# Backward pass of a recurrent memory attention: dV's and dK's sum folded into dQ's bank, and a shorter set-up of the backward loop

## The chip, the cores and the metric

The kernel runs on one core of a Trainium2 chip. The metric is the device time of one execution in microseconds (us). TensorE (PE in the profile) multiplies matrices, with weight loads listed apart as PEld; VectorE (DVE), ScalarE (ACT) and GpSimd (POOL) do elementwise work; SyncE (SP) and GpSimd issue most of the DMAs. SBUF is the on-chip memory, and PSUM holds the results of TensorE.

## The reference

A layer with adaptive layer norms, an attention over segments with a carried memory, and a gated feed-forward network; the kernel returns its output and eleven gradients. What matters here is the attention. 2048 rows of 512 are cut into 64 segments of 32 rows. Each segment sees 8 memory rows and its own 32, and its first 8 output rows are the next segment's memory:

```python
for s in range(n_seg):
    h = concatenate([mem, xs], axis=1)                  # 40 rows of 512
    q, k, v = (einsum('btd,dhe->bhte', h, W) for W in (Wq, Wk, Wv))   # 32 heads of 128
    p = softmax(where(mask, einsum('bhqe,bhke->bhqk', q, k) * scale, -1e9))
    o = einsum('bhte,hed->btd', einsum('bhqk,bhke->bhqe', p, v), Wo)
    mem = o[:, :M, :]
    outs.append(o[:, M:, :])
```

The backward pass walks the segments from 63 down to 0. For each it needs dO from dy and Wo, then dV, dP, dS, dK and dQ, and from these the gradient of the 40 input rows, dh = dV Wv^T + dK Wk^T + dQ Wq^T. The first 8 rows of dh are the gradient of the memory, and so a part of dy of the segment that is handled next. That makes the loop a chain.

## The kernel before

`phase4` is the backward loop over the 64 segments, the stretch from about 1513 to 2500 us of the profile. The order of all engines' instructions in the loop is the order of the program text (`pin`). The heads lie three to a group of 128 columns, in 11 groups, of which 120 columns are used: three times 32 rows, then three times the last 8 rows of the 40. Columns 120 to 127 of each group are padding.

One segment goes like this. `col_pass` multiplies dy (`dyT`) with `WoT` into `pass_ps`, which is copied to `RAd`; eight transposes (`turn_ps`) bring it to `dOT`. GpSimd also copies `RAd` to rows 0 to 95 of `dOst` (L1693). Rows 96 to 119 of `dOst` are dO of the last 8 rows of each head. These come from `RBd`, which holds dO of the last 8 rows of four segments, by three small DMAs on GpSimd's queue (`dO_tails`, L1579). Then come the products for dV, dP, dS, dK and dQ (`g_ps`, `dp_ps`, `tps`).

The sum dh is made in two banks of PSUM. `dht` puts the products of dV with `WvT` and of dK with `WkT` into `dh_ps`, 128 x 512. Each head's product fills a strip of 32 partitions (the first 32 rows of the 40), four heads side by side, so that the four strips have still to be added. `dht_pairs` puts those of dQ with `WqT` into `dhq_ps`, 128 x 256: here two strips hold the left half of the 512 columns and two the right half. `pair_mm` issues four such matmuls at a time, one for each strip. Both banks are split into two bf16 tiles, a high part on ScalarE and the remainder on VectorE, so that TensorE can add the strips without loss: `fold_split` puts the parts of `dh_ps` into the tile `dST` (L312, L313), and `split_pair` makes `dh_hi` (L230) and `dh_lo` (L232) from `dhq_ps`. `fold_sum` (L323) then adds everything into `dh_ft`, 128 x 4 x 32, which is dh transposed: eight matmuls for the parts of `dh_ps` with the selector `foldsel` (it adds four strips), eight for those of `dhq_ps` with `foldhalf` (it adds two). ScalarE copies the memory rows of `dh_ft` to the next `dyT` (L1767), and the next segment's `col_pass` can begin.

Between the split and the fold stands other work of TensorE where there is some: a piece of the product of the last 8 rows of four segments (`TailRows`, `dh_tps`), of 16 or 24 matmuls, from the fifth segment of the loop on. In one segment of four, eight matmuls of that product's own fold (`dh_b_ft`) follow it, also at L323.

Before the loop, tiles are cleared. `ptiles` clears whole tiles with GpSimd memsets (L1463): `dS`, `dOst`, `dKT`, `dQT`, `Qst` and `Kst`, 128 x 1408 each. VectorE clears `dOT` (L1468). SP loads `OT`, `Pst` and `VT` of segments 63 and 62 (L1547, L1550), and `Qst` and `Kst` of segment 63 once these are cleared (L1564). GpSimd goes on with `to_heads` (L65), which writes the last rows into `dOT`; then the three DMAs of `dO_tails`, a DMA of eight zero rows to `DHA` (L1582), and the first copies to `dOst`. The scheduler chooses the place of what stands outside the pinned loop.

Of the kernel before, what the change touches and what calls it, by code (L numbers as in the profile page):

```python
# [40 lines left out]
class K:  # L41
# [1389 lines left out]
    def phase4(self):  # L1431
        nc, tc, cfg, io = self.nc, self.tc, self.cfg, self.io
        D, DC, H, E, L, M, T, G, NS = cfg.D, cfg.DC, cfg.H, cfg.E, cfg.L, cfg.M, cfg.T, cfg.G, cfg.NS
        GW = 128
# [4 lines left out]
        with self.p4_ctx as ctx:  # L1439
# [6 lines left out]
            psp = ctx.enter_context(tc.tile_pool(name="p4ps", bufs=6, space=PSUM, reuse_waits="tile"))  # L1446
# [11 lines left out]
            def ptiles(name, n, zero=True):  # L1458
                ts = []
                for i in range(n):  # L1460
                    t = pt.tile([128, G * GW], BF16, name=f"{name}{i}")
                    if zero:
                        nc.gpsimd.memset(t[:], 0.0)  # L1463
                    ts.append(t)
                return ts
# [3 lines left out]
            RAd = pt.tile([128, 8 * 128], BF16, name="RAd")  # L1469
            RBds = [pt.tile([128, 8 * 128], BF16, name=f"RBd{i}") for i in range(2)]  # L1470
            btd = pt.tile([128, 8, 128], BF16, name="btd")
            dSs = ptiles("dS", 1)
            dSTs = ptiles("dST", 1, zero=False)
            dOst_t = ptiles("dOst", 1)[0]
            dXTs = {nm: ptiles(nm, n, zero=nm != "dVT") for nm, n in (("dVT", 1), ("dKT", 1), ("dQT", 1))}

            def part3(t, pi):
                return t[:, pi * PW:min((pi + 1) * PW, G * GW)].rearrange("p (g x) -> p g x", x=GW)
# [17 lines left out]
            def to_heads(eng, src, i0, n, r0, w, o):  # L1496

                b = 0 if w == 32 else 96
                s4 = src.rearrange("p i (j r) -> p i j r", r=32)
                d = dOT[:, 120 * i0:120 * (i0 + n)].rearrange("p (i x) -> p i x", x=120)[:, :, b:b + 3 * w]  # L1500
                self.evac(eng, d.rearrange("p i (j r) -> p i j r", r=w), s4[:, :, 0:3, o:o + w])
                for g in range(3):
                    lo, hi = max(3 * g, i0), min(3 * g + 3, i0 + n, 8)
                    if lo < hi:
                        d = dOT[:, 960 + 120 * g + b + w * (lo - 3 * g):960 + 120 * g + b + w * (hi - 3 * g)]
                        self.evac(eng, d.rearrange("p (i r) -> p i r", r=w), s4[:, lo - i0:hi - i0, 3, o:o + w])
# [9 lines left out]
            def proj_b(t, hf, parts=1):  # L1516
                ps = psb.tile([128, 512], F32, name="pass_ps", tag="dh")

                def part(k):
                    self.col_pass(psp, WoT, hf, lambda c: dbs[t][:, c, :, :].rearrange("p s q -> p (s q)"), None, None, ps,  # L1520
                                  range(k * DC // parts, (k + 1) * DC // parts))

                part(0)

                def rest():
                    for k in range(1, parts):
                        part(k)
                    return lambda: self.evac(("act", "dve")[hf], RBds[t % 2][:, 512 * hf:512 * hf + 512], ps[:])

                return rest  # L1530

            def turn_b(t):
                tps = [self.turn_half(psp, RBds[t % 2], hf) for hf in range(2)]

                def f():
                    for hf in range(2):
                        self.evac(("act", "dve")[hf], btd[:, 4 * hf:4 * hf + 4, :], tps[hf][:])
                return f
# [31 lines left out]
            get_loads(NS - 1)  # L1570
            for hf in range(2):
                proj_b(NS // 4 - 1, hf)()()
            turn_b(NS // 4 - 1)()
            to_heads("pool", btd[:], 0, 8, 32, 8, 24)

            def dO_tails(s):
                for j in range(3):
                    o = 32 * j + 8 * (s % 4)
                    nc.gpsimd.dma_start(dOst_t[96 + 8 * j:104 + 8 * j, 0:1024], RBds[(s // 4) % 2][o:o + 8, :])  # L1579

            dO_tails(NS - 1)
            nc.gpsimd.dma_start(self.DHA[NS, 0:M, :], dSs[0][0:M, 0:D])  # L1582
            nseg_t = 128 // T
            row_stores = []

            def store_rows_x(left):
                while len(row_stores) > left:
                    row_stores.pop(0)()
# [3 lines left out]
            i0 = len(self.traced())  # L1592
            for s in reversed(range(NS)):
# [12 lines left out]
                dS, dST, dOst = dSs[0], dSTs[0], dOst_t  # L1606
                dVT, dKT, dQT = dXTs["dVT"][0], dXTs["dKT"][0], dXTs["dQT"][0]
# [74 lines left out]
                def dht_pairs(X, WT):  # L1682
                    ps = psp.tile([128, 256], F32, name="dhq_ps", tag="p")
                    off = lambda h: (h // 3) * GW + (h % 3) * 32
                    for n in range(H // 2):
                        hs = (2 * n, 2 * n + 1)
                        self.pair_mm(ps, [X[:, off(h):off(h) + 32] for h in hs], [WT[:, h, :] for h in hs], n, H // 2)
                    return ps

                for a, n, eng in ((0, 4, "dve"), (4, 2, "act"), (6, 2, "act")):  # L1690
# [66 lines left out]
                dht(dVT, WvT, 2)  # L1757
                parts = self.fold_split(sb2, dh_ps[0], "dh", dST)
                pair = self.split_pair(sb2, dht_pairs(dQT, WqT), "dh")
                tail.collect(s % nseg_t, [dVT, dKT, dQT])  # L1760
                tail.chunk()
                if split:
                    self.pop_later()
                store_rows_x(2)
                ft = self.fold_sum(psp, parts, "dh", "p", pair)
                if dyT_next is not None:
                    nc.scalar.activation(dyT_next[:, :, 0:M], ft[:, :, 0:M], AF.Copy)  # L1767
                g = s // 4
# [428 lines left out]
```

## Time and profile before

| | us |
|---|---|
| median of three runs | 3073.68 (3072.13 to 3074.03) |
| the profiled execution, its own time | 3071.52 |
| its span, first to last instruction | 3069.7 |
| TensorE busy in the span | 2972.8 |
| VectorE, ScalarE, GpSimd busy | 1604.4, 1285.6, 1212.6 |
| mean granted clock of TensorE | 0.991 |

The span and what lies around it (1.8 us) make the profiled execution's time, which is 2.16 us below the median of the runs. In the lists of the trace, a line gives the start in us, the duration, the engine and the line of the kernel, the operation with out<-in, the shape, the count, and in brackets the idle time of the engine before it with what ended that time. Neighbours of one kind are merged into one line (x16 is 16 instructions), whose duration runs from the first start to the last end. The chain lists only what set the end: each step follows from what released it.

### The profile page before, as it was taken

The page shows a single profiled execution, that of the slowest core. Times are in us where ns is not written, and L with a number is a line of the kernel's source. Part 1 is how long each engine was busy: PE and PEld are TensorE (multiplying, and loading weights), DVE is VectorE, ACT ScalarE, POOL GpSimd, SP SyncE. Part 2 cuts the span into 40 slices and gives each one's busy share as a digit, 9 for nine tenths or more (in the row PEclk, how much of TensorE's full clock was granted, in tenths as well). Part 3 has the DMA queues.
Part 4 walks back from the last instruction along what each step waited for, and adds up shares of the span by engine and source line. Part 5 has one row for each costly group of instructions (what it writes and reads, how often), then busy time and mean ns, then how long its engine had stood idle before and what let it go on. Part 6 is the DMA issues. An engine that isn't in the chain of part 4 may idle for free. (4 is left out here: it accounts for less than half of the span.)

```text
span 3069.7 us, 106628 instructions
## 1 busy us (share of the span) xinstructions
PE 2972.8 (97%) x44289; PEld 1859.2 (61%) x44289; DVE 1604.4 (52%) x3746; ACT 1285.6 (42%) x3179; POOL 1212.6 (40%) x2640
## 2 busy tenths in 40 slices
PE   6999999999998899989899999999999999999999
PEld 3666666666665444445567777777777754445454
DVE  5556656656655788732255555555555532322221
ACT  2555555555555433322255555555555520111011
POOL 2554555555544222211244444444444422333321
PEclk8999999999999999999999999999999999999999
DMA  9887887887887899997599999999999998666574
GB/s 303 216 220 203 219 212 208 210 217 208 213 207 253 197 229 231 226 285 242 169 246 245 245 244 247 246 248 246 244 246 252 247 280 270 205 197 220 184 243 143
DMA packets 839319, 703.53 MB, mean 229 GB/s; under 512 B 539730, under 2 KB 711794, under 8 KB 837940
## 3 DMA queue, kind: packets, MB, share of 16 engines
q1 hardware_dynamic: 713668, 486.69, 62.9%
q0 software_dynamic: 54512, 148.63, 15.5%
q10 hardware_dynamic: 70656, 61.41, 6.4%
q8 instruction: 348, 5.70, 0.8%
q14 instruction: 135, 1.11, 0.1%
HBM read 294.93 MB, written 276.35 MB: 186 GB/s over the span
## 5 line engine op out<-in xcount | busy, mean ns | idle before, releaser
L1987 PE MATMUL gps<-rows,hrows 128*128 128x512 bf16 (+2 forms) x2160 | 417.5, 355 | 0.0
L1987 PEld LDWEIGHTS <-hrows 128*128 128x128 bf16 x2160 | 211.2, 98 | 204.6
L1693 POOL COPY dOst<-RAd 96x512 bf16<-96x512 bf16 x128 | 75.1, 611 | 309.3 <-DVE RAd L63 309.3
L63 DVE CAST ot<-gps 128x512 bf16<-128x512 f32 (+3 forms) x76 | 48.1, 633 | 284.2 <-PE gps L1987 192.5
L656 PE MATMUL pass_ps<-Wv,hT 128*32 128x512 bf16 (+2 forms) x2304 | 188.2, 357 | 0.0
L61 ACT ACTIVATE ot<-gps 128x512 bf16<-128x512 f32 (+3 forms) x75 | 41.3, 551 | 350.6 <-PE gps L1987 228.0
L255 PEld LDWEIGHTS <-hT 128*32 128x32 bf16 x4096 | 125.1, 97 | 95.8 <-DMA Wq<-in_A_Wq_dram 6.2
L1991 POOL DMA_DIRECT2D out_dram<-ot x108 | 81.3, 753 | 251.0 <-DVE ot L63 134.0
L942 POOL TENSOR_TENSOR Pst<-Pst,rden 120x1408 bf16<-120x1408 bf16 x63 | 159.8, 2537 | 39.1 <-issue 23.3
L61 ACT ACTIVATE dVT<-g_ps 128x480 bf16<-128x480 f32 (+1 forms) x192 | 104.7, 545 | 97.1 <-PE g_ps L1649 96.6
L63 DVE CAST Vst<-pass_ps 96x512 bf16<-96x512 f32 x128 | 87.3, 682 | 107.4 <-ACT RBv L61 97.7
L215 PE MATMUL dh_ps<-WvT,dVT 128*32 128x512 bf16 x2048 | 133.6, 381 | 0.1
L255 PE MATMUL pass_ps<-Wq,hT 128*32 128x512 bf16 x2048 | 125.6, 383 | 6.0 <-DMA Wq<-in_A_Wq_dram 6.0
L2001 PE MATMUL gps5o<-WoT,rows 128*128 128x512 bf16 x592 | 128.3, 379 | 1.6 <-DMA rows<-OSR 1.6
L223 PE MATMUL at_ps<-Wo,OT 128*32 128x256 bf16 x4096 | 124.8, 275 | 2.6 <-DMA Wo<-in_A_Wo_dram 2.6
L656 PE MATMUL pass_ps<-Wv,hb 128*32 128x512 bf16 (+2 forms) x636 | 127.2, 345 | 0.0
L255 PE MATMUL pass_ps<-Wk,hT 128*32 128x512 bf16 x2048 | 124.3, 380 | 1.7 <-POOL hT L545 1.1
L731 POOL DMA_DIRECT2D Vst<-RBv x192 | 99.4, 523 | 64.6 <-ACT ET L778 39.9
L255 PE MATMUL pass_ps<-WoT,dyT 128*32 128x256 bf16 (+1 forms) x3072 | 122.4, 308 | 0.9 <-ACT dyT L1767 0.9
L223 PE MATMUL dhq_ps<-WqT,dQT 128*32 128x256 bf16 x4096 | 122.9, 273 | 0.0
L215 PE MATMUL dh_ps<-WkT,dKT 128*32 128x512 bf16 x2048 | 122.3, 380 | 0.0
L223 PEld LDWEIGHTS <-dQT 128*32 128x32 bf16 x4096 | 109.7, 97 | 15.7
(413 smaller groups left out, 7004.2 us busy)
## 6 DMA issues: line engine op xcount, KB each, us to landing
OSR<-Ost SPq DMA_DIRECT2D x64, 352.0 KB
OT<-OT SPq DMA_DIRECT2D x64, 352.0 KB
VT<-VTr SPq DMA_DIRECT2D x64, 352.0 KB
PS<-Pst SPq DMA_DIRECT2D x64, 352.0 KB
OT_l<-OT SPq DMA_DIRECT2D x64, 352.0 KB
Pst_l<-PS SPq DMA_DIRECT2D x64, 352.0 KB
VT_l<-VT SPq DMA_DIRECT2D x64, 352.0 KB
DVR<-rows_x POOLq DMA_DIRECT2D x64, 352.0 KB, 6.0
```

The lines of the kernel that those rows point to most:

```text
L61: return nc.scalar.activation(out, in_, AF.Copy)
L63: return nc.vector.tensor_copy(out, in_)
L215: self.nc.tensor.matmul(ps[32 * j:32 * j + 32, :], lhsT=lhsT, rhs=w, start=(n < 4), stop=(n >= total - 4), tile_position=(0, 32 * j))
L223: nc.tensor.matmul(ps[32 * j:32 * j + 32, :], lhsT=x[k], rhs=w[k][:, 256 * d:256 * d + 256], start=(n == 0), stop=(n == total - 1), tile_p ...
L255: self.nc.tensor.matmul(ps[32 * j:32 * j + 32, :], lhsT=lhs(c), rhs=rhs, start=(c == 0), stop=(c == DC - 1), tile_position=(0, 32 * j))
L656: nc.tensor.matmul(ps[32 * j:32 * j + 32, o * E:(o + n) * E], lhsT=lhsT, rhs=wc[:, 3 * a + hl:3 * (a + n - 1) + hl + 1:3, :], start=(c == ...
L731: nc.gpsimd.dma_start(Vst[96 + 8 * j:104 + 8 * j, :], rb[32 * j + o:32 * j + o + 8, :])
L942: nc.gpsimd.tensor_tensor(Pst[0:120, :, :], Pst[0:120, :, :], rden[:, :].unsqueeze(2).to_broadcast([120, G, 128]), op=ALU.mult)
L1693: nc.gpsimd.tensor_copy(dOst[0:96, 512 * hf:512 * hf + 512], RAd[0:96, 512 * hf:512 * hf + 512])
L1987: nc.tensor.matmul(ps[:, 0:ng * E], lhsT=hrows[:, tp_, c * 128:(c + 1) * 128], rhs=rows[:, tp_, 0:ng * E], start=(tp_ == 0), stop=(tp_ == ...
L1991: nc.gpsimd.dma_start(outw[c * 128:(c + 1) * 128, h0:h0 + 3 * (ng - 1) + 1:3, :], ot[:, 0:ng * E].rearrange("p (h e) -> p h e", e=E))
L2001: nc.tensor.matmul(pss[gg][:], lhsT=src[0][:, src[1], gg * E:(gg + 1) * E], rhs=dyrows[:, tp_, :], start=(tp_ == order[0]), stop=(tp_ == o ...
```

## The change

The four products of `foldsel` with the two parts of `dh_ps` now go into `dhq_ps`, as a seventeenth round of `pair_mm` behind the sixteen of dQ. The split of `dhq_ps` thus holds the whole sum, and `sum_pair` folds it with eight matmuls in place of sixteen. Before the loop, `dS`, `dKT` and `dQT` are no longer cleared as a whole, only at their padding columns (and `dS` at the rows that the zero rows of `DHA` are read from); `dOst` is cleared by VectorE; and `dO_tails` is moved ahead of `turn_b` and `to_heads`, with GpSimd's order pinned there. In the built program, SP's loads of `Qst` and `Kst` then stand third and fourth, ahead of the first load of `VT`.

```diff
-            dSs = ptiles("dS", 1)
+            dSs = ptiles("dS", 1, zero=False)
             dSTs = ptiles("dST", 1, zero=False)
-            dOst_t = ptiles("dOst", 1)[0]
-            dXTs = {nm: ptiles(nm, n, zero=nm != "dVT") for nm, n in (("dVT", 1), ("dKT", 1), ("dQT", 1))}
+            dOst_t = ptiles("dOst", 1, zero=False)[0]
+            nc.vector.memset(dOst_t[:], 0.0)
+            dXTs = {nm: ptiles(nm, n, zero=False) for nm, n in (("dVT", 1), ("dKT", 1), ("dQT", 1))}
+            nc.vector.memset(dSs[0][0:32, 0:D], 0.0)
+            for t in (dSs[0], dXTs["dKT"][0], dXTs["dQT"][0]):
+                nc.vector.memset(t[:].rearrange("p (g x) -> p g x", x=GW)[:, :, 120:GW], 0.0)
...
-            turn_b(NS // 4 - 1)()
-            to_heads("pool", btd[:], 0, 8, 32, 8, 24)
...
+            i0 = len(self.traced())
             dO_tails(NS - 1)
+            turn_b(NS // 4 - 1)()
+            to_heads("pool", btd[:], 0, 8, 32, 8, 24)
             nc.gpsimd.dma_start(self.DHA[NS, 0:M, :], dSs[0][0:M, 0:D])
+            self.pin(i0, [mybir.EngineType.Pool])
...
                     for n in range(H // 2):
                         hs = (2 * n, 2 * n + 1)
-                        self.pair_mm(ps, [X[:, off(h):off(h) + 32] for h in hs], [WT[:, h, :] for h in hs], n, H // 2)
+                        self.pair_mm(ps, [X[:, off(h):off(h) + 32] for h in hs], [WT[:, h, :] for h in hs], n, H // 2 + 1)
+                    self.pair_mm(ps, [self.foldsel[:, :]] * 2, parts, H // 2, H // 2 + 1)
                     return ps
...
-                ft = self.fold_sum(psp, parts, "dh", "p", pair)
+                ft = self.sum_pair(psp, pair, "dh", "p")
```

`sum_pair` exists already:

```python
ft = psp.tile([128, self.cfg.DC, 32], F32, name=name + "_ft", tag=tag)
for i in range(2):
    for c in range(self.cfg.DC):
        self.nc.tensor.matmul(ft[:, c, :], lhsT=parts[i][:, (c % 2) * 128:(c % 2) * 128 + 128],
                              rhs=self.foldhalf[:, c // 2, :], start=(i == 0 and c == 0), stop=(i == 1),
                              skip_group_check=True)
```

## The prediction

> **What bounds the kernel now.** I read the page first, then the chain of the backward loop, then the list of instructions at the end of one segment, and last the list and the DMA view of the loop's start.
>
> ```profile
> PE 2972.8 (97%) x44289; PEld 1859.2 (61%) x44289; DVE 1604.4 (52%) x3746; ACT 1285.6 (42%) x3179; POOL 1212.6 (40%) x2640
> ```
>
> TensorE is busy for 97% of the span, twice any other engine. In the loop it hardly ever waits; the chain of a segment's end is TensorE alone:
>
> ```profile
> 1702.60 1.75 PE dhq_ps L223 x64
> 1704.34 0.86 PE dh_tps L215 x16
> 1705.21 0.50 PE dh_ft L323 x16
> 1705.70 2.71 PE pass_ps L255 x64
> ```
>
> So what changes TensorE's own work here is paid or saved in full, unless the split of `dhq_ps` (ScalarE, then VectorE) becomes later than TensorE's other work. Both are in the list of the same segment:
>
> ```profile
> 1703.34 0.69 DVE L313 TENSOR_TENSOR dST<-dh_ps,dST 128x512 bf16<-128x512 f32 x1 [2.42 <-ACT dST L312]
> ...
> 1704.17 1.04 PE L215 MATMUL dh_tps<-WqT,dh_tail 128*32 128x512 bf16 x16
> 1704.40 0.38 ACT L230 ACTIVATE dh_hi<-dhq_ps 128x256 bf16<-128x256 f32 x1 [1.09 <-PE dhq_ps L223]
> ...
> 1705.45 0.25 PE L323 MATMUL dh_ft<-foldsel,dh_lo 128*128 128x32 bf16 x4
> ...
> 1705.63 0.62 PE L255 MATMUL pass_ps<-WoT,dyb 128*32 128x512 bf16 x8
> ```
>
> From the start of `dh_hi` to the next pass it takes 1.23 us. The loop's first segment, which has no `dh_tps` in between, shows how short that can get when the split alone decides: 1.09 us.
>
> ```profile
> 1539.51 0.38 ACT L230 ACTIVATE dh_hi<-dhq_ps 128x256 bf16<-128x256 f32 x1 [1.09 <-PE dhq_ps L223]
> 1539.93 0.42 DVE L232 TENSOR_TENSOR dh_lo<-dhq_ps,dh_hi 128x256 bf16<-128x256 f32 x1 [0.78 <-ACT dh_hi L230]
> ...
> 1540.41 0.27 PE L323 MATMUL dh_ft<-foldsel,dh_lo 128*128 128x32 bf16 x4 [0.19 <-DVE dh_lo L232]
> ...
> 1540.60 0.61 PE L255 MATMUL pass_ps<-WoT,dyb 128*32 128x512 bf16 x8
> ```
>
> At the loop's start TensorE stands still for 8 us, and the three DMAs of `dO_tails` end it:
>
> ```profile
> 1513.45 1.27 POOL L1463 MEMSET dS<- 128x1408 bf16 x1 [0.32 <-PE wtp L1400]
> ...
> 1514.04 0.61 DVE L1468 MEMSET dOT<- 128x664 uint32 x1
> ...
> 1519.51 1.27 POOL L1463 MEMSET Kst<- 128x1408 bf16 x1
> ...
> 1520.81 0.33 SPq L1564 DMA_DIRECT2D Kst<-KST  x1
> ...
> 1521.84 1.53 POOL L1579 DMA_DIRECT2D dOst<-RBd  x3
> ...
> 1527.48 0.56 PE L1649 MATMUL g_ps<-Pst_l,dOst 128*128 128x120 bf16 x4 [7.99 <-DMA dOst<-RBd]
> ```
>
> **The fold, segment by segment.** Removed are 8 of 16 fold matmuls. In the list they start 0.025 us apart (four `dh_hi` and four `dh_lo` starts lie 0.10 apart), so TensorE saves 8 x 0.025 = 0.20 us. Added are four products of 32 x 256, in the form of the 64 before them; 64 take 1.75 us, so one round of four takes 1.75 / 16 = 0.11 us. No product of `foldsel` with 256 columns is in the trace; its bounds are 0.11 us if the four strips work abreast like dQ's, and 4 x 0.11 = 0.44 us if they go one after another. I take 0.11, the row of the same shape and strips. TensorE's own work falls by 0.09 us.
>
> The split starts later by the same 0.11 us, as it now waits for the extra round. That has to fit in the room between TensorE's path and the split's. With a `dh_tps` of 16 and nothing more, the room is 1.23 - 1.09 = 0.14 us, of which 0.11 are used: the segment gains 0.04 (0.146 - 0.110 with the starts to the ns), not 0.09. Where eight matmuls of `dh_b_ft` or eight more of `dh_tps` stand between, there are over 0.2 us more room and the segment gains 0.09. Of four segments two are of each sort: 2 x 0.036 + 2 x 0.09 = 0.25 us. 60 segments have such work: 15 x 0.25 = 3.8 us less. The first four have none, and there the later split costs its 0.11 in full: 0.4 us more. **The loop gains 3.3 us.**
>
> The new wait is that the second product needs VectorE's part in `dST` (L313). It ends at 1704.03 in the list. The round before the products begins at 1704.06 and they follow 0.11 later, at 1704.17, which leaves 0.14; with 0.06 from an end on VectorE to the matmul that waits for it (1540.35 to 1540.41), 0.08 to 0.09 us are left. The figure is the same to 0.01 in all 64 segments. Behind it would queue everything of TensorE; a delay beyond 0.09 us costs its length in each segment.
>
> The other engines do the same as before. SP's and GpSimd's queues in the loop are unchanged, and q1, the hardware queue of SP's loads, is empty for some 3 us of each segment (1713.0 to 1716.0 for instance, by the packets), so a segment shorter by 0.06 us finds its loads in time. If that cover were gone, at most the 3.3 us would be lost.
>
> **The start.** Removed from GpSimd are four memsets of 1.27 us at 1.21 distance, 4.9 us. VectorE takes on the clearing of `dOst` (128 x 704 against `dOT`'s 128 x 664 in 0.61: 0.65 us), of 32 x 256 in `dS` (0.24 by the same rate), and three padding strips of 44 elements (0.04 by that rate, at most the 0.21 of a 128 x 128 copy of that engine): 1.0 to 1.5 us. VectorE has 1.07 us free between the memset of `dOT` and the copy to `RBd` at 1515.72, so `RBd` is later by 0 to 0.4 us; behind it queue `turn_ps`, `btd` and the first pass, all of them ahead of the 8 us of idle time that covers this. GpSimd would clear `Qst` and `Kst` by 1515.9, start `dO_tails` when `RBd` is whole, at about 1516.7, issue the last of the three at 1517.7, and have `to_heads` (1.2 us), the zero rows (0.5) and the copies to `dOst` (1.2) done by 1521.1. By issue times alone the tails are 5.1 us sooner.
>
> What they gain depends on how the DMA engines order them. SP's loads of `Qst` and `Kst` wait for the memsets and are now issued about 4.8 us earlier, so that all eight loads of 330 to 352 KB are in the queue before the last tail is. The rows that bear on it are the stores of `DKR` and `DQR`, of one size and from the same queue as the tails:
>
> ```profile
> DKR<-rows_x POOLq DMA_DIRECT2D x58, 352.0 KB, 5.2
> DQR<-rows_x POOLq DMA_DIRECT2D x58, 352.0 KB, 3.6
> ...
> dOst<-RBd POOLq DMA_DIRECT2D x174, 16.0 KB, 5.0
> ```
>
> The `DKR` issued at 1709.11 is behind three loads of SP (1706.2 to 1709.0), and its first packet starts at 1712.9, 3.8 us later, just as the last packet of those loads is served; the `DQR` issued at 1713.94 finds q1 empty, and its first packet starts 1.1 us later. At the loop's start it is the same: one DMA engine of the sixteen works off loads without a break, 0.112 us a packet, until 1526.37, and serves the tails' semaphores from 1526.38 on, though the other engines had them from 1523.1. So DMAs are served here nearly in the order of arrival, and the tails stay last. The bytes ahead of them are the same as before; only the pauses before `Qst` and `Kst` (under 1 us for a usual engine, none for the slowest) fall away. By this the gain lies between -0.5 (another engine is slow) and 1.5 us; I take 0.8.
>
> The Trainium skill says otherwise ("DMA: Bandwidth & Descriptors", "Queues, rings and completion order"): each DMA engine takes turns between the queues that have work, packet by packet. By this rule the tails would pass the loads, and the sum would be 7.6 us less in place of the 4.1 of the rows; the `DKR` row speaks against it, and the rows decide here.
>
> TensorE's granted clock adds scatter to the start: it is 0.50 from 1521.17 to 1531.41, so 3.9 us of work after the wait run at half speed, and 2 us are lost. The clock's changes lie on a grid of 3.41 us (10.24 is three steps), and where the wait ends on that grid is chance. I leave this loss as it is, and give the range 1 us for it.
>
> **Sum.** 3.3 + 0.8 = 4.1 us less. The profiled execution would go from 3071.52 to 3067.4; against the median of 3073.68 it is 3069.6 us. What a measurement of this kernel can tell from no change is about 0.2%, 6.1 us, so the forecast is a gain below that bound.
>
> **Rivals.** First, the tails pass the loads. Then they land some 2 us after their issue (a store issued at 1512.59 into an empty queue landed at 1514.55), by about 1520.7; the copies to `dOst` end at 1521.1, and next late is `VT`, now the fifth load, whose last share would come when the fifth load's came before, at 1523.4. The start gains 4.3 us in place of 0.8: 3073.68 - 3.3 - 4.3 = 3066.1 us. The 5.0 us of the tails' usual landing speak against it. Chance 0.24.
>
> Second, the later split eats the gain in more segments than I count, by a fold that restarts more slowly after a wait, or by 0.05 us more at the first product. Then the loop gains nothing: 3072.9 us. The room of 0.036 us in half the segments speaks for it. Chance 0.11.
>
> Third, slower: the four products do not run abreast, as all four carry one stationary matrix. They then take 0.44 us: TensorE's path grows by 0.24 us in 30 segments, the split's by 0.29 in 30 and 0.44 in four: 7.2 + 8.7 + 1.8 = 17.7 us more, 3090.6 with the start's gain. It decides from 0.05 us a segment on, where the 3.3 us are used up. Against it: dQ's own rounds use one matrix for two strips and show 0.11. Chance 0.10, with any other loss.
>
> **How the numbers follow.** The forecast keeps 0.55. The range goes from the first rival with the clock's scatter, 3065.3, to the second, 3073.6; it leaves out the third and a tenth of the rest. Faster than the bound: most of the first rival and a tenth of the forecast, 0.26. Slower: 0.09. Within it: 0.65.
>
> **What would show it.** In the list of a steady segment: four `dhq_ps<-dST,foldsel` within 0.11 us, no wait of TensorE ahead of them, `dh_hi` 0.11 later, eight `dh_ft`, and periods shorter by 0.04 or 0.09 us, in the first four longer by 0.11. At the start: GpSimd's tails at 1516.7 and TensorE's wait ending within 1.5 us of 1527.3. If it ends before 1524, the order of arrival is wrong; if the products are spread over 0.4 us, the third rival is right.

## The result, and the profile after

| | before | after |
|---|---|---|
| median, us | 3073.80 (3068.44 to 3080.26, 18 runs) | 3068.34 (3064.43 to 3071.88, 18 runs) |
| profiled execution, its own time | 3071.52 | 3067.55 |
| its span | 3069.7 | 3065.8 |

The ratio of the times is 0.9979, with a 95% interval of 0.9973 to 0.9985: 4.6 to 8.3 us less, with 6.5 us in the middle; the two medians are 5.5 us apart. The forecast was 4.1 us less, which lies just outside that interval. The median lies 1.3 us below the forecast of 3069.6 and inside its range, and the gain sits at the bound of 0.2% that the prediction named.

The page shows what TensorE no longer does. Its first line, of the kernel after:

```profile
PE 2965.5 (97%) x43957; PEld 1854.3 (60%) x44033; DVE 1606.1 (52%) x3751; ACT 1286.4 (42%) x3179; POOL 1209.6 (39%) x2636
```

Eight fold matmuls less and four products more in 64 segments make 256 weight loads less, and PEld is down by 256, from 44289 to 44033. (PE is down by more, since some matmul records are missing.) TensorE is still the only engine near its limit.

**The loop.** The chain at the end of a segment, of after, is the one that the prediction showed of before (columns: start, us, engine and group):

```profile
1700.49 1.86 PE dhq_ps L223 x68
1702.34 0.86 PE dh_tps L215 x16
1703.21 0.35 PE dh_ft L240 x8
1703.56 2.71 PE pass_ps L255 x64
```

Sixty-eight products take 1.86 us where 64 took 1.75: the extra round costs 0.11. Eight fold matmuls cost 0.35 on the chain where sixteen cost 0.50. The list of the same segment tells how close the split now is:

```profile
1701.23 0.69 DVE L313 TENSOR_TENSOR dST<-dh_ps,dST 128x512 bf16<-128x512 f32 x1 [2.42 <-ACT dST L312]
...
1702.06 0.28 PE L223 MATMUL dhq_ps<-dST,foldsel 128*32 128x256 bf16 x4
...
1702.17 1.04 PE L215 MATMUL dh_tps<-WqT,dh_tail 128*32 128x512 bf16 x16
1702.39 0.38 ACT L230 ACTIVATE dh_hi<-dhq_ps 128x256 bf16<-128x256 f32 x1 [1.20 <-PE dhq_ps L223]
...
1702.81 0.43 DVE L232 TENSOR_TENSOR dh_lo<-dhq_ps,dh_hi 128x256 bf16<-128x256 f32 x1 [0.89 <-ACT dh_hi L230]
...
1703.29 0.27 PE L240 MATMUL dh_ft<-foldsel,dh_lo 128*128 128x32 bf16 x4
...
1703.49 0.62 PE L255 MATMUL pass_ps<-WoT,dyb 128*32 128x512 bf16 x8
```

The four products take 0.28 us from first start to last end, one of them alone takes 0.27, and the next work starts 0.11 us behind the first of them: they run side by side. No idle time stands in brackets ahead of them, so VectorE's part (L313, which ends at 1701.92) isn't late; in the whole loop TensorE has no idle time over 0.15 us ahead of these products. From `dh_hi` to the next pass it is now 1.10 us (1702.39 to 1703.49), which is the 1.09 at which the split alone decides: the room is used up.

**The start.** The lines of after:

```profile
1515.94 0.35 SPq L1568 DMA_DIRECT2D Qst<-QST  x1
...
1516.22 0.65 DVE L1475 MEMSET dOst<- 128x704 uint32 x1
1516.86 0.27 DVE L1477 MEMSET dS<- 32x256 uint32 x1
...
1517.09 0.10 DVE L1479 MEMSET dKT<- 128x44 uint32 x1
...
1518.49 1.53 POOL L1581 DMA_DIRECT2D dOst<-RBd  x3 [1.40 <-ACT btd L61]
1518.88 0.43 SPq L1554 DMA_DIRECT2D VT_l<-VT  x1
...
1521.22 1.36 POOL L1700 COPY dOst<-RAd 96x512 bf16<-96x512 bf16 x2
...
1525.91 0.56 PE L1655 MATMUL g_ps<-Pst_l,dOst 128*128 128x120 bf16 x4 [4.92 <-DMA dOst<-RBd]
```

TensorE's wait is 4.92 us where it was 7.99, and the same three tail DMAs end it. The first is issued between the last two loads of segment 62, the second and third behind both: the third at 1519.52, 0.64 after the second load of `VT`.

### The profile page after: what moved, and what is told of

Its sections match the earlier page's. It is cut to its first block, busy times and chain, and to the rows that moved or that the text cites. A ratio compares the mean times of both kernels' runs of the same rounds, so it can differ in the third digit from the quotient of the medians.

```text
span 3065.8 us, 106040 instructions
## 1 busy us (share of the span) xinstructions
PE 2965.5 (97%) x43957; PEld 1854.3 (60%) x44033; DVE 1606.1 (52%) x3751; ACT 1286.4 (42%) x3179; POOL 1209.6 (39%) x2636
## 4 chain that ended last, share of the span: by engine, by line
PE 86%; DMA 5%; issue 4%; DVE 2%; POOL 1%; ACT 1%; SPq 1%; another core or an unknown queue 0%; ACTq 0%; POOLq 0%; DVEq 0%
PE pass_ps L255 14%; PE gps L1994 9%; PE dh_ps L215 8%; PE g_ps L1655 6%; PE pass_ps L656 5%; PE gps5o L2008 4%; PE dhq_ps L223 4%; PE at_ps L223 4%; PE gps L1334 3%; PE mm L1178 3%; PE dh_tps L215 3%; PE turn_ps L766 2%; PE dp_ps L1632 2%; PE tps L1563 2%; PE st_ps L776 1%
## 5 line engine op out<-in xcount | busy, mean ns | idle before, releaser
L341 POOL DMA_DIRECT2D AOA<-at_rb x64 | 36.3, 567 | 213.4 <-DVE at_rb L337 213.4
```

## The experiments

One sort of number serves all of them, read from the lists. The work ahead of the loop ends at different times in different executions, whatever the kernel: the last transpose of the weights (`wtp`, L1400) began anywhere from 1509.8 to 1516.9 us in the fourteen profiles. So the wait's end is counted from there. "To dQ" runs from the wait's end to the first dQ product of the first segment; it holds what a halved clock costs. "Loop" runs from that product to the first one of the 64th segment, and a period is the time between the same two products of neighbouring segments. A DMA is spread over the sixteen DMA engines, and each engine marks when its share has landed; TensorE waits for the last of the sixteen marks.

| profile | wait | wait's end after `wtp` | to dQ | loop |
|---|---|---|---|---|
| before | 7.99 | 14.32 | 10.06 | 952.54 |
| e11, before again | 7.12 | 13.44 | 10.03 | 952.73 |
| e1, fold only | 7.23 | 13.55 | 10.54 | 948.92 |
| e5, clearing as before | 6.37 | 12.70 | 9.83 | 949.15 |
| e6, tails' place as before | 5.93 | 12.28 | 10.33 | 950.06 |
| after | 4.92 | 11.27 | 9.50 | 949.86 |
| e10, after again | 4.71 | 11.07 | 9.66 | 948.98 |
| e2, start only | 4.96 | 11.31 | 9.82 | 952.68 |
| e4, other pieces | 5.30 | 11.65 | 9.90 | 948.16 |
| e3, segment 62's loads late | 3.99 | 10.34 | 9.84 | 951.44 |
| e7, loads in another order | 3.89 | 10.24 | 10.96 | 949.39 |
| e8, e7 with e4's pieces | 3.91 | 10.26 | 9.86 | 950.33 |
| e9, loads behind the tails, e4's pieces | 1.10 | 7.46 | 8.34 | 948.31 |
| e12, loads behind the tails | 0.91 | 7.27 | 8.53 | 948.97 |

### The two parts by themselves: e1 and e2

e1 is the kernel before with the fold alone:

```diff
+                        self.pair_mm(ps, ..., n, H // 2 + 1)
+                    self.pair_mm(ps, [self.foldsel[:, :]] * 2, parts, H // 2, H // 2 + 1)
...
+                ft = self.sum_pair(psp, pair, "dh", "p")
```

> The kernel before with the fold's part of the change alone; the start is left as it was. Theory (TensorE's own work falls by 0.09 us a segment, but where only a dh_tps of 16 stands between, the later split leaves 0.04): 3.3 us less than the kernel before, periods shorter by 0.04 us in half of the segments and by 0.09 in the other half, the first four longer by 0.11, and the start's wait of 8 us as before (6 to 8). Rival (the fold gives nothing, the start all): no change in the loop's periods on balance, and 0 us. Rival (the fold gives 0.09 everywhere): 5 us less.

Measured: 3069.51 us against 3072.85 before, ratio 0.9989 (0.9980 to 0.9998), 3.3 us less. Four neighbouring periods of the steady loop sum to 60.386 us where before has 60.641: 15.323, 15.263, 14.913 and 14.887 in place of 15.414, 15.357, 14.950 and 14.923. That is 0.09 less in two and 0.037 less in two, as the room foretold. The first periods are 14.966, 14.966, 14.560 and 14.887 for 14.857, 14.857, 14.450 and 14.776, each 0.11 longer.

e2 is the kernel after without the fold, so that only the start differs from before:

```diff
-                    self.pair_mm(ps, [self.foldsel[:, :]] * 2, parts, H // 2, H // 2 + 1)
...
-                ft = self.sum_pair(psp, pair, "dh", "p")
+                ft = self.fold_sum(psp, parts, "dh", "p", pair)
```

> The kernel before with the start's part alone (memsets, tails first, loads of Qst and Kst earlier); the fold of sixteen stays. The prediction's figure was 0.8 us less, as the tails would stay behind all eight loads. The theory after seeing the two traces: the tails are served in order of arrival, ahead of the last two or three loads, so that TensorE's wait falls from 8 to about 5 us, and the time by 3 us, with 1 us of scatter from the clock. Rival (the 3 us between the traces are chance of one slow DMA engine): wait of 6.5 to 8 us here, time less by under 1.5 us. The loop's periods are those of before.

Measured: 3071.43 against 3072.85, ratio 0.9996 (0.9987 to 1.0005). The time alone can't tell this from no change, nor from the 3 us that the trace gives. In the trace it has the start of after and the loop of before (60.641 per four periods). Its wait, in the list of TensorE:

```profile
1526.75 0.47 PE L1655 MATMUL g_ps<-Pst_l,dOst 128*128 128x120 bf16 x4 [4.96 <-DMA dOst<-RBd]
```

So the two parts don't touch each other: fold and loop, start and wait.

### The start taken apart: e5 and e6

e5 is after with the six GpSimd memsets of before; the tails keep their new place, ahead of `turn_b` and `to_heads`:

```diff
-            dSs = ptiles("dS", 1, zero=False)
+            dSs = ptiles("dS", 1)
...
-            dOst_t = ptiles("dOst", 1, zero=False)[0]
-            nc.vector.memset(dOst_t[:], 0.0)
+            dOst_t = ptiles("dOst", 1)[0]
```

> The changed kernel with the six whole-tile memsets back on GpSimd; only dO's tail rows stay ahead of turn_b and to_heads. The tails then start when the sixth memset ends, 1.1 us sooner than in the kernel before, and the loads of Qst and Kst are issued where they were, ahead of the tails. Order of arrival: the tails stay behind all eight loads, TensorE's wait is 6 to 8 us, as in the two runs that had the old start (8.0 and 7.2). If it is moving the tails ahead of to_heads that counts: wait of about 5 us.

e6 is after with the tails' old place and without the pinned order; the clearing stays short:

```diff
+            turn_b(NS // 4 - 1)()
+            to_heads("pool", btd[:], 0, 8, 32, 8, 24)
...
             dO_tails(NS - 1)
-            turn_b(NS // 4 - 1)()
-            to_heads("pool", btd[:], 0, 8, 32, 8, 24)
```

> The changed kernel with turn_b and to_heads put back ahead of the tails in the program; the clearing is that of the change. The tails start 1 to 1.5 us later than in the changed kernel, so that all eight loads are ahead of them by arrival. If arrival decides: the wait is that of the changed kernel plus 1 to 2 us, 5.5 to 7 us. If the saved memsets are all that counts: 5 us.

Measured, one execution each: 3066.38 and 3071.77 us; e6's work ahead of the loop ended late (`wtp` at 1516.6), so the waits say more than these times. TensorE's waits, e5's line first, then e6's:

```profile
1525.37 0.56 PE L1651 MATMUL g_ps<-Pst_l,dOst 128*128 128x120 bf16 x4 [6.37 <-DMA dOst<-RBd]
```

```profile
1528.89 0.56 PE L1653 MATMUL g_ps<-Pst_l,dOst 128*128 128x120 bf16 x4 [5.93 <-DMA dOst<-RBd]
```

Counted from `wtp`, the mean end of the three starts of before (before, e11, e1) is 13.77 and that of the three starts of after (after, e10, e2) is 11.22. e5 lies 1.1 below the first, e6 1.5. Each step alone thus gives a share, and the two make up the 2.55 of both; but each rests on one execution, and the three starts of before lie up to 0.9 apart. In e6 the scheduler put the third tail behind the last head copies, at 1522.76, 1.9 us after the last load's issue. It landed behind that load on the median engine, 11.0 us after `wtp` against 10.7, while the first two tails, issued up to 0.85 us after the load, landed ahead of it, at 9.9 and 10.4.

### What is ahead of the tails: e3, e7, e9, e12

The theory was that DMAs are served in the order in which they reach the DMA engines, so that what counts is how many loads are ahead of the tails. Its rival was that the queues take turns. e3 issues the loads of segment 62 only after the reload of `Qst` in the first segment:

```diff
-                if s > 0:
+                if 0 < s < NS - 1:
                     get_loads(s - 1)
...
+                if s == NS - 1:
+                    get_loads(s - 1)
```

> The changed kernel, but the loads of segment 62 (OT, Pst, VT) are issued after the reload of Qst in the first segment, not before the loop's first products. Order of arrival: only five loads are ahead of the tails in place of seven or eight, so they land by about 1521.5 to 1523 on the changed kernel's time scale (1525.7 there), TensorE's wait falls from 4.9 to some 2 us, and the kernel is 2 to 3 us faster than the changed one, if the later loads reach segment 62 in time; the next late things are the copies to dOst (1522.6) and VT (the fifth load). Turns between the queues, packet by packet: the loads never held the tails up, the wait stays at 4.5 to 5 us and the time at that of the changed kernel.

Measured: 3067.05 against 3072.85, ratio 0.9983 (0.9974 to 0.9992), 5.8 us less than before, hardly more than the change alone brings. The wait:

```profile
1527.21 0.37 PE L1655 MATMUL g_ps<-Pst_l,dOst 128*128 128x120 bf16 x4 [3.99 <-DMA dOst<-RBd]
```

It fell to 3.99 us and not to the 2 us that were expected, and the late loads lengthened the first two periods by 0.5 and 0.1. The completion times settle what the tails waited for. On the median of the sixteen DMA engines, the five loads of segment 63 were complete 2.9, 3.8, 5.5, 6.9 and 8.0 us after `wtp`, and the tails at 8.2, 8.4 and 8.7, directly behind the last of them. They were issued from 1520.72 on, at 3.9, with three of these loads unfinished. Had the queues taken turns, they would have passed `Kst` and `VT`. They passed neither, and it was their data that waited, not only the marks: the first of the tails' data packets started 3.15 us after the first issue, against 1.1 us in e12.

e7 puts `VT` ahead of `Qst` and `Kst`, with these two cleared by VectorE after the copy to `RBd` and SP's order pinned:

```diff
-            load_rows(Qst_t, self.QST, NS - 1)
-            load_rows(Kst_t, self.KST, NS - 1)
...
+            for t, dram in ((Qst_t, self.QST), (Kst_t, self.KST)):
+                nc.vector.memset(t[:], 0.0)
+                load_rows(t, dram, NS - 1)
```

> The changed kernel with SP's loads in the order OT, Pst, VT, Qst, Kst, then those of segment 62; Qst and Kst are cleared by VectorE behind the copy to RBd, so that their loads, and all that follow on SP's queue, are issued at about the time of the tails. Order of arrival: OT, Pst, VT and at most Qst are ahead of the tails, which land some 3 to 4 us after their issue in place of 6 to 7; TensorE's wait falls from 5 to 2 to 2.5 us (the copies to dOst are next late), and the kernel is 2 to 3 us faster than the changed one. Turns between the queues: no difference.

Measured: 3063.82 against 3072.36, ratio 0.9973 (0.9963 to 0.9982), 8.5 us less. The wait is 3.89 us, where 2 to 2.5 had been expected. The first tail was issued at 1513.66, `Qst` at 1513.84, `Kst` at 1514.58, the third tail at 1514.69. The medians of the landings are: first tail 1517.2, `Qst` 1517.5, second tail 1517.8, `Kst` 1519.0, third tail 1519.2. This is the order of issue across two queues. Yet the order doesn't explain the length: when the first tail was issued, `VT` was 0.9 us from landing (1514.57) and nothing else was ahead, and still the tail took 3.5 us, where e12's took 1.6. `Qst`, issued 0.18 us behind it, was in the queue beside it; so a load just behind a tail seems to delay it too (3.4 us in e8, whose start is the same). The chain of e7 shows the third tail as what TensorE waited for:

```profile
1514.69 5.11 DMA dOst<-RBd
1519.80 0.25 issue
1520.04 0.56 PE g_ps L1658 x4
```

e9 and e12 draw the conclusion: `Qst`, `Kst`, the fourth part of dy and the loads of segment 62 are all issued behind the first segment's own dO work, so that only `OT`, `Pst` and `VT` of segment 63 are ahead of the tails. e9 has e4's pieces as well, e12 hasn't:

```diff
-                if s == NS - 1:
-                    get_da(s // 4 - 1)
-                if s > 0:
+                if 0 < s < NS - 1:
                     get_loads(s - 1)
...
+                if s == NS - 1:
+                    for t, dram in ((Qst_t, self.QST), (Kst_t, self.KST)):
+                        nc.vector.memset(t[:], 0.0)
+                        load_rows(t, dram, s)
+                    get_da(s // 4 - 1)
+                    get_loads(s - 1)
```

> As the run with reordered loads and pieces, but Qst and Kst are cleared and loaded only after the first copies to dOT, and the loads of segment 62 behind them: of SP's loads only OT, Pst and VT are ahead of the tails. Order of arrival: the tails land some 3 us after their first issue, TensorE's wait falls from 3.9 us to about 2, ended by GpSimd's copies to dOst, and the time by 1 to 2 us against that run: 9 to 11 us faster than the kernel before. If the wait stays at 3.9 us, the order of arrival is not the cause, and some 4 us is what these DMAs take anyway.

> The changed kernel with its own pieces of the last rows' product, and only the order of the start altered: Qst, Kst, the fourth part of dy and the loads of segment 62 are issued after dO's tail rows. Theory (DMAs are served in the order in which they arrive, so the tails should find only the loads of segment 63's OT, Pst and VT ahead of them): TensorE's wait ends 1.0 to 1.5 us after it begins (4.7 to 5.0 in the changed kernel), the granted clock does not fall to a half after it (3.0 us of half speed, 1.5 us of loss, in the changed kernel), and the periods stay at 60.39 us per four segments: 3.6 + 1.5 = 5.1 us below the changed kernel, 11.5 to 12 us below the kernel before, and 0.7 us above the version that had the other pieces too. Rival (the lasting full clock in the earlier run was chance, a matter of where the wait fell on the clock's grid): the wait is as short, but about 3.4 us at half speed follow it, and 3.6 us are gained on the changed kernel. Rival (turns between queues): the wait is short as well, since nothing else is then in the queue; this run does not tell that one apart.

Measured: e9 3058.97 against 3073.24, ratio 0.9952 (0.9938 to 0.9966), 14.3 us less and more than the 9 to 11 expected; e12 3062.23 against 3074.14, ratio 0.9962 (0.9948 to 0.9975), 11.9 us less as expected. The list of e12's start:

```profile
1514.87 1.53 POOL L1581 DMA_DIRECT2D dOst<-RBd  x3 [3.90 <-DMA Pst_l<-PS]
...
1517.60 1.17 POOL L1698 COPY dOst<-RAd 96x512 bf16<-96x512 bf16 x2
...
1518.28 0.38 PE L1653 MATMUL g_ps<-Pst_l,dOst 128*128 128x120 bf16 x4 [0.91 <-POOL dOst L1698]
...
1518.53 0.35 SPq L1568 DMA_DIRECT2D Qst<-QST  x1
```

The tails land 1.6 us after their issue on the median engine, and the wait is 0.91 us, put down to GpSimd's copy to `dOst`; the tails' last share landed at 1518.03, only 0.2 us before the first copy's end, and in e9 it is still the tails that end the wait of 1.10 us. The loads come in time all the same; the periods of the first segments (14.97, 14.97, 14.56, 14.88) are those of after. The rows of TensorE's clock tell of a second gain. The windows of after, then of e12 (columns: window, length, busy time and count of PE, PEld, DVE, ACT and POOL, granted clock, DMA share, GB/s):

```profile
1525.00:1530.00 5.00, 4.09 (x53) 3.57 (x57) 1.28 (x3) 1.52 (x3) 1.09 (x5) 0.66 0.07 24
1530.00:1535.00 5.00, 5.00 (x95) 3.52 (x87) 3.02 (x6) 3.46 (x8) 3.01 (x7) 1.00 0.32 77
```

```profile
1515.00:1520.00 5.00, 4.04 (x85) 2.94 (x75) 3.72 (x13) 2.37 (x8) 3.80 (x11) 1.00 0.27 69
1520.00:1525.00 5.00, 5.00 (x86) 3.66 (x88) 4.03 (x9) 3.44 (x9) 1.55 (x7) 1.00 1.03 285
```

In after the clock is halved from 1525.16 to 1528.58. In e12 it is full throughout, and so it is in e9. Against e10, the way from the wait's end to dQ is 1.1 us shorter in e12 and 1.3 in e9. All twelve profiles with a wait of 3.9 us or more have the half clock, the two with 0.9 and 1.1 don't. That fits a clock that falls with idle time; it wasn't tried by itself. Against the profile of e10, e12's wait and clock are worth 3.8 + 1.1 = 4.9 us, where 5.1 had been expected. e9 is the fastest of all versions, 7.4 us below after (3066.40, e10).

### The room in the loop: e4 and e8

The list of after shows segments with 16 matmuls between split and fold at their limit, and others with 24 with room to spare. e4 moves four matmuls from one to another:

```diff
-            tail = TailRows(..., (16, 24, 8, 8, 16, 8, 16), home=dSs[0])
+            tail = TailRows(..., (16, 20, 8, 8, 20, 8, 16), home=dSs[0])
```

> The changed kernel with four of the tail product's matmuls moved from the piece of 24 to one piece of 16 in each four segments (16, 20, 8, 8, 20, 8, 16). Theory of the room: behind 20 matmuls the split is no longer late, so the segment that had 16 loses a stall of 0.054 us and the one that had 24 keeps its 0.09: over the two segments TensorE's work is the same, and the sum of four periods falls by 0.05 us, 0.8 us in all, which is seen in the trace's periods and hardly in the times. Rival (the split is not what binds in the segments with 16): the sum of four periods is unchanged.

> As the run with SP's loads reordered, and with the pieces 16, 20, 8, 8, 20, 8, 16 of the tail product. Expected as that run, and 0.8 us less: 3 to 4 us faster than the changed kernel, 8 to 10 us faster than the kernel before.

Measured: e4 3066.32 against 3072.85, ratio 0.9978 (0.9969 to 0.9987); e8, which adds the pieces to e7, 3063.05 against 3072.36, ratio 0.9968 (0.9957 to 0.9980). Two of four periods change to 15.05 and 15.07 (from 15.26 and 14.91) and the sum of four falls from 60.386 to 60.333, by 0.05: 0.8 us in the loop. That is too small for the times but plain in the periods.

### The two kernels again: e10 and e11

Both were run again without an edit, for the scatter of the start.

> The changed kernel once more, beside the run before it: TensorE's wait of 4.9 to 5.3 us, typical periods as in its first trace, and 4 to 7 us faster than the kernel before.

> The kernel before once more, for a third look at the old start: a wait of 7 to 8 us.

Measured: e10 3066.40 against 3073.24, ratio 0.9981 (0.9972 to 0.9990); e11, one execution, 3070.93. The waits are 4.71 and 7.12. The first profile of before, on which the prediction was built, had the longest wait of the three of its kind (before, e1, e11), by 0.8 us.

## Why the prediction came out as it did

**The loop was right, term by term.** The round costs 0.11, the products run abreast, and 0.037 is gained in half the segments and 0.09 in the others. The loop's length over the seven profiles with the new fold and otherwise the loop of after (e1, after, e5, e6, e7, e10, e12) has a mean of 949.3 us, and over the three with the old one 952.65: 3.3 us. Single values lie up to 0.7 from their mean, since single periods are longer now and then: in after one of 15.80 stands in place of 14.81. By the periods alone it is 15 x 0.256 - 4 x 0.11 = 3.4. The second and the third rival are thereby refuted: the round of `dhq_ps<-dST,foldsel` cost 0.11 us, not 0.44, and only the first four segments, as foretold, lost their gain.

**The start's gain was mis-sized: 0.8 was taken, 3.1 measured.** Of the 3.1, 2.55 is the earlier end of the wait and 0.55 the shorter way to dQ (9.66 in place of 10.21 in the means of three), as less of the halved clock lies over work (2.7 to 3.4 us behind the wait's end in place of 3.9 to 4.9). The prediction took the clock's loss as unchanged. The median fell into the prediction's range because the range reaches down to the first rival; the sum itself was 2.4 us short. (The bounds as written lie 0.8 and 0.7 us from the rivals' times, not the 1 us that was named, which changes nothing here.)

Its single steps held on their way. The work ahead of the loop ended 1.48 us later in this execution than in that of before, and with this taken off, the copy to `RBd` began 0.07 later (0 to 0.4 was given), the tails were issued at 1517.0 (1516.7) and the copies to `dOst` ended at 1521.1 (1521.1). VectorE's clearing took 0.65, 0.27 and three times 0.10.

The step that failed is "DMAs are served here nearly in the order of arrival, and the tails stay last". The first half is what the landings of e3 and e7 show. The second half wasn't true. In after and e10 the third tail was issued 0.64 us after the last load and landed before it: on the median engine 10.6 us after `wtp` in both, with the second `VT` at 11.1. (In e2 SP issued the last two loads late, `VT` 0.49 us behind the third tail; the tail landed at 10.6, `VT` at 11.5.) The difference is larger on the slowest of the engines, and TensorE waits for that one: the last share of the third tail came at 11.0 on the mean of three, that of `VT` at 12.2. In the three starts of before the tails had followed `Kst` on the slowest engine and were complete 0.5 us behind it, at 13.6. Had they followed `VT` in the same manner, they would have come at 12.7, 0.9 earlier than before: about the 0.8 of the prediction. By this working the other 1.7 us come from not standing behind `VT`, and on the slowest engine not behind part of the load ahead of it. e6, where the third tail did stay last on the median engine, ended its wait 1.5 us earlier than before, so the passing may be worth only the remaining 1.1.

The profile's packets add what the prediction saw on one engine only. The last data packet of the tails was served 11.2 to 11.6 us after `wtp` in the three starts of before and 9.8 to 10.3 in those of after, 1.4 earlier in the mean; but TensorE waited 2.0 to 2.7 us more for the marks in before and 1.0 to 1.3 in after. Nearly half of the 2.55 us is thus the shorter wait for the slowest engine's mark, not earlier data.

**The first rival was half right.** It let the tails pass all the loads, land some 2 us after their issue and end the wait 4.3 us earlier. They passed one or two, landed 4.7 to 5.8 us after their issue (medians over the engines), and the wait ended 2.55 us earlier. The rule of turns behind it, which the Trainium skill states ("DMA: Bandwidth & Descriptors", "Queues, rings and completion order"), doesn't describe these rows: by it the tails of e3 would have overtaken `Kst`. Nor does a strict order of issue: the first tail of e7 took 1.9 us longer than that of e12 with only a load behind it added, and a tail may overtake a load that was issued 0.6 us before it, as here, or 1.1 us (the second tail of e2 and the load of `OT` ahead of it), while those of e3, issued 1.0 us after `VT`, stayed behind it. Neither of the prediction's own signs was met, an end of the wait within 1.5 us of 1527.3 for the forecast (by its own gain of 0.8 it should have written 1526.7), or one before 1524 for the rival: with the 1.48 taken off it is 1524.4, between the two theories' figures, so that the result alone could not have told them apart. How deep a DMA engine works ahead in one queue, which would give the rule between the two, stays open.

**The sum.** 3.3 in the loop and 3.1 at the start make 6.4 us. The stretch behind the loop, whose code is the same, was 0.7 us longer in the mean of the profiles with the new fold than in those with the old one (580.1 against 579.4, with a scatter of about as much); whether that is chance stays open. With it the sum is 5.7; measured were 4.6 to 8.3.

## What to carry to other kernels

Before an addition moves ahead of a split, measure the slack from the split to the work that covers it: here 0.14 us took 0.11, and where the cover ends the rest has to be paid in full. A small DMA that a bound engine waits for should be issued well before the large loads, not only earlier: 0.18 us ahead was not enough (e7), and holding back loads that are not yet needed (e12) brought another 4.9 us by the trace, to the 6.5 of the change. A wait taken away from TensorE can also be worth the halved clock that follows it, so a sum over a stall needs both terms.

## What the runs showed of the hardware

- DMAs of two queues landed in the order of their issue in e7 and e3, with 16 KB pieces between loads of 330 KB; in other starts loads were overtaken by tails issued up to 1.1 us after them (e2), though not always at 1.0 (e3) and not at 1.9 (e6). A tail of 16 KB took 1.6 us with little ahead of it, 3.5 with one load issued just behind it (e7), and 5.8 with a full queue (medians over the engines).
- The last of the sixteen DMA engines finished the third tail 1.1 to 1.9 us after the median engine in the starts of before, and 0.3 to 0.5 after it in those of after. The last mark came 1.8 to 2.5 us after the tails' last data packet in those of before, 0.8 to 1.1 in those of after.
- TensorE's granted clock was 0.5 for 3.4, 6.8 or 10.2 us in all twelve profiles with an idle time of 3.9 us or more at the start, and never below 1 there in the two with 0.9 and 1.1 us.
- The same code ahead of the loop ended up to 7 us apart in fourteen executions, which is more than the whole change. A difference of 1 to 3 us was to be read from the traces, counted from a mark near by.
